# One PSUM tile for each unit, and no product under 64 columns, in a stacked RWKV-7 and mixture-of-experts kernel

## The chip, the cores and the metric

The kernel runs on one core of a Trainium2 chip. The metric is the device time of one execution in microseconds (us). Engines are called as in the profile: PE is the tensor engine's products, PEld its weight loads, DVE the vector engine, ACT the scalar engine, POOL the general engine, SP the engine that issues most transfers. [...]

## The reference

Two blocks run one after the other. The first is a linear recurrence over 768 tokens with 4 batches x 8 heads of dimension 40, and the second sends each token through one of 8 experts.

```python
# attention: for every token t, batch b and head h (state is 40 x 40)
y[t]  = r[t] @ state
Sa    = state @ a[t]
state = state * w[t][:, None] - outer(Sa, b[t]) + outer(v[t], k[t])
# bridge: x = y of all heads side by side, 3072 rows of 320
# experts
logits = x @ w_gate                      # 8 experts
e = argmax(logits); gate = softmax(logits)[e]
out = gate * (relu(x @ w1[e]) @ w2[e])   # hidden size 1024
```

## The kernel before

Tokens are taken in 12 steps of 64. In a step the recurrence becomes a set of small matrix products and a triangular system, which is solved by five doubling levels. The 32 (batch, head) pairs are held as two **units** (`s` = 0, 1) of 16 each: 8 groups `g` times 2 halves `par` of the partitions. A set of products for one unit is therefore 16 products, and since a float32 product leaves two records in the trace, 32 records.

Two streams are woven on PE. `systems` prepares the triangular systems of the next step; `rest` finishes the current step. After every two system products some products of `rest` are issued, in proportion. [...]

```python
def chain(u):                                   # systems, one unit
    return ([lambda: gram(u, 0), lambda: gram(u, 1)] + [lambda k=k: level(u, k) for k in range(5)]
            + [lambda: couple(u), lambda: whole(u)])

def rest(us, nx, before):                       # us: both units of this step
    ps = [right(us), solve(us)] + [lambda u=u: zgram(u) for u in us]
    if before: ps += [(emit(before),)]          # rows of x and logits of the step before
    ps += [lambda u=u: atv(u) for u in nx]
    if not last: ps += [(state(us),)]
    ps += [y_state(us), (y_rest(us),)]
    if not last: ps += [turned(us)]
    return ps
```

PSUM tiles come from two rings of two double banks each: `wide` for the systems (and, with the other tag, for z and atv), `banks` for pairs of smaller results. One call of `banks` allocates one tile and hands out its two halves, one for each unit.

```python
def wide(name, tag="sys"):
    t = pp.tile([128, 2, 512], F32, name=name, tag=tag, bufs=2)
    return t[:].rearrange("q b (g x) -> q (b g) x", x=128)

def banks(name, w):
    t = pp.tile([128, 2, 512], F32, name=name, tag="rest", bufs=2)
    return [t[:, i, : G * w].rearrange("q (g x) -> q g x", x=w) for i in range(2)]

def parted(ps):                                 # PE waits until its writes so far have landed
    nc.scalar.copy(seen[64:65], ps[64:65, G - 1, 0:1])
```

The users of `banks` have the form of `right`, which makes q from two sums of products. The sums come from different halves of the array's rows into the same bank[...].

```python
def right(us):
    pss = banks("ps_q", D)
    for u, ps in zip(us, pss):
        ...
        if c:
            yield [lambda g=g, par=par: mm(
                ps[own(par), g, :], d["ai"][own(par, D), g, :T2], st_r[s][0][own(par, D), g, :D],
                start=(g == 0), stop=False, free=True) for g, par in HD], lambda ps=ps: parted(ps)
    for u, ps in zip(us, pss):
        def end():
            t = d["q"] = q_r[s][0]
            nc.scalar.activation(t[:, :, :D], ps[:], AF.Copy, scale=-1.0)
        yield [lambda g=g, par=par: mm(
            ps[own(par), g, :], d["GT"][oth(par), g, :], d["vu"][par][oth(par), g, :D],
            start=(c == 0), free=True) for g, par in HD], end
# solve (ps_uT), state (ps_s), turned (ps_S), y_state + y_rest (ps_y), emit (ps_x): likewise
```

Evacuations that matter: gram is read by DVE (`pair`) and then ACT (`off`, `nkb`, `GT`); a level by ACT (`pair`), DVE adds, and DVE transposes the copy into the next level's weights `N`; z and atv by four ACT copies each; the levels end with `D`, a DVE transpose that the coupling product `couple` needs.

```python
def zgram(u):                                   # atv has the same form
    ps = wide("ps_z", "rest")
    ts = [lambda g=g, par=par: mm(ps[own(par), g, : T2 + D], d["uT"][oth(par, D), g, :], d["ri"][oth(par, D), g, :])
          for g, par in HD]
    def end():
        for par in range(2):
            nc.scalar.copy(d["vu"][par][own(par), :, :D], ps[own(par), :, T2 : T2 + D])
        for par in range(2):
            t = d["az"][par]
            nc.scalar.copy(t[own(par)], ps[own(par), :, :T2])
            nc.gpsimd.tensor_tensor(t[:], t[:], up64[:, None, :].to_broadcast([128, G, T2]), op=ALU.mult)
    return ts, end
```

The expert block follows, with PSUM tiles of its own; the change does not touch it.

Of the kernel before, what the change touches and what calls it, by code (L numbers as in the profile page):

```python
# [21 lines left out]
def kernel(  # L22
# [102 lines left out]
    with tc.tile_pool(name="ring", bufs=1) as ring, \  # L125
# [16 lines left out]
        def oth(par, n=T2):  # L142
            return slice((1 - par) * 64, (1 - par) * 64 + n)
# [51 lines left out]
        def preset_rest():  # L195
            for s in range(NB2):
                nc.gpsimd.memset(off_r[s][0][:], 0.0)
                nc.gpsimd.tensor_copy(ri_r[s][0][:, :, T2:], i40[:, None, :].to_broadcast([128, G, D]))
                nc.gpsimd.tensor_copy(x_r[s][0][:], i64[:, None, :].to_broadcast([128, G, T2]))

            for t in [r[i] for i in range(2) for r in nkb_r[0] + nkb_r[1] + vu_r[0] + vu_r[1]] + [r[0] for r in q_r + st_r + s_r]:
                nc.gpsimd.memset(t[:, :, D:], 0.0)
            for s in range(NB2):
                nc.gpsimd.memset(kb_r[s][1][:], 0.0)
                for r in (ai_r, ri_r):
                    nc.gpsimd.tensor_copy(r[s][1][:, :, T2:], i40[:, None, :].to_broadcast([128, G, D]))
# [8 lines left out]
                    iw[own(par, D), :, 2 * D :], moe_w_gate.rearrange("(p a e) x -> a e p x", p=NP, a=2)[par],  # L215
                )

        def wide(name, tag="sys"):

            t = pp.tile([128, 2, 512], F32, name=name, tag=tag, bufs=2)  # L220
            return t[:].rearrange("q b (g x) -> q (b g) x", x=128)

        def banks(name, w):

            t = pp.tile([128, 2, 512], F32, name=name, tag="rest", bufs=2)
            return [t[:, i, : G * w].rearrange("q (g x) -> q g x", x=w) for i in range(2)]

        def mm(out_, lhs, rhs, start=True, stop=True, free=False):
            nc.tensor.matmul(out_, lhsT=lhs, rhs=rhs, start=start, stop=stop, skip_group_check=free)  # L229
# [103 lines left out]
        def atv(u):  # L333

            c, s = u
            d = units[u]
            ps = wide("ps_atv", "rest")
            ts = [lambda g=g, par=par: mm(ps[oth(par), g, : T2 + D], d["v"][oth(par, D), g, :], d["ri"][oth(par, D), g, :])
                  for g, par in HD]

            def end():
                d["vu"], d["az"] = [vu_r[par][s][c % 2] for par in range(2)], stack("az", s, T2)
                for par in range(2):
                    nc.scalar.copy(d["vu"][par][oth(par), :, :D], ps[oth(par), :, T2 : T2 + D])
                for par in range(2):
                    nc.scalar.copy(d["az"][par][oth(par)], ps[oth(par), :, :T2])
            return ts, end


# [16 lines left out]
        def level(u, k):  # L366
            c, s = u
            d = units[u]
            ps = wide("ps_lv")
            N, pair = d["N"], d["pair"]  # L370
            rhs = d["nt0"] if k == 0 else pair[:] if k < 4 else pair[:, 2:]
            at = slice(0, T2) if k == 0 else slice(0, T2 + 32) if k < 4 else slice(T2, T2 + 32)
            ts = [lambda g=g, par=par: mm(
                ps[own(par), g, at].rearrange("q (a t) -> q a t", t=32), N[own(par), g].rearrange("q a t -> q (a t)"), rhs[own(par), :, g, :])
                for g, par in HD]

            def end():
                new = pair if k == 0 else new_pair(d, s)
                if k < 4:
                    nc.scalar.copy(parts(new[:, :2]), ps[:, :, :T2].rearrange("q g (a t) -> q g a t", a=2))  # L380
                    new_n(d, s, new[:, :2])
                if k > 0:
                    nc.vector.tensor_tensor(new[:, 2], ps[:, :, T2 : T2 + 32], pair[:, 2], op=ALU.add)
                if k == 4:
                    D_ = d["D"] = sb.tile([128, 1, G, 32], F32, name=f"D{s}")
                    nc.vector.transpose(flat(D_[:]), flat(new[:, 2:]))
                    t = d["TT"] = sb.tile([128, 2, G, 32], F32, name=f"TT{s}")
                    nc.gpsimd.tensor_tensor(
                        t[:], new[:, 2:].to_broadcast([128, 2, G, 32]), blk[:, :, None, :].to_broadcast([128, 2, G, 32]),
                        op=ALU.mult,  # L390
                    )
            return ts, end

        def couple(u):

            c, s = u
            d = units[u]
            ps = wide("ps_y21")
            ts = [lambda g=g, par=par: mm(ps[own(par), g, :32], d["off"][own(par), g, :], d["D"][own(par), 0, g, :])
                  for g, par in HD]  # L400

            def end():
                x = d["x"] = x_r[s][0]
                for par in range(2):
                    qs = slice(par * 64 + 32, par * 64 + 64)
                    nc.scalar.copy(x[qs, :, :32], ps[qs, :, :32])
            return ts, end
# [16 lines left out]

        def right(us):

            pss = banks("ps_q", D)
            for u, ps in zip(us, pss):
                c, s = u
                d = units[u]  # L430
                if c:
                    yield [lambda g=g, par=par: mm(
                        ps[own(par), g, :], d["ai"][own(par, D), g, :T2], st_r[s][0][own(par, D), g, :D],
                        start=(g == 0), stop=False, free=True) for g, par in HD], lambda ps=ps: parted(ps)
            for u, ps in zip(us, pss):
                c, s = u
                d = units[u]

                def end():
                    t = d["q"] = q_r[s][0]  # L440
                    nc.scalar.activation(t[:, :, :D], ps[:], AF.Copy, scale=-1.0)  # L441
                yield [lambda g=g, par=par: mm(
                    ps[own(par), g, :], d["GT"][oth(par), g, :], d["vu"][par][oth(par), g, :D],
                    start=(c == 0), free=True) for g, par in HD], end

        def solve(us):
# [11 lines left out]
        def zgram(u):  # L458

            c, s = u  # L460
            d = units[u]
            ps = wide("ps_z", "rest")
            ts = [lambda g=g, par=par: mm(ps[own(par), g, : T2 + D], d["uT"][oth(par, D), g, :], d["ri"][oth(par, D), g, :])
                  for g, par in HD]

            def end():
                for par in range(2):
                    nc.scalar.copy(d["vu"][par][own(par), :, :D], ps[own(par), :, T2 : T2 + D])
                for par in range(2):
                    t = d["az"][par]  # L470
                    nc.scalar.copy(t[own(par)], ps[own(par), :, :T2])  # L471
                    nc.gpsimd.tensor_tensor(t[:], t[:], up64[:, None, :].to_broadcast([128, G, T2]), op=ALU.mult)  # L472
            return ts, end

# [16 lines left out]

        def turned(us):

            for u, ps in zip(us, banks("ps_S", D)):
                c, s = u

                def end():
                    nc.scalar.copy(s_r[s][0][:, :, :D], ps[:])
                yield [lambda g=g, par=par: mm(ps[oth(par), g, :], st_r[s][0][own(par, D), g, :], i40[own(par, D), :])
                       for g, par in HD], end  # L500

        def y_state(us):
# [21 lines left out]

        def emit(us):

            for u, ps in zip(us, banks("ps_x", 2 * NP * D // G + 2 * E)):
                c, s = u
                d = units[u]
                ps = ps.rearrange("t g x -> t (g x)")[:, : NP * (2 * D + E)].rearrange("t (p x) -> t p x", p=NP)  # L530

                def end():
                    xr = sb.tile([128, DX], F32, name="xr", bufs=2)
                    lg = sb.tile([128, E], F32, name="lg", bufs=2)
                    nc.scalar.copy(xr[:, :Dm].rearrange("t (p e) -> t p e", p=NP), ps[:, :, : 2 * D])  # L535
                    nc.gpsimd.tensor_copy(xr[:, Dm:], xr[:, Dm - 64 : Dm])
                    nc.vector.tensor_reduce(lg[:], ps[:, :, 2 * D :].rearrange("t p x -> t x p"), axis=AX, op=ALU.add)  # L537
                    nc.vector.tensor_scalar_mul(lgn[:, s * NS + c, :], lg[:], -1.0)
                    for b2 in range(2):
                        r0 = (2 * s + b2) * S + c * T2  # L540
                        nc.sync.dma_start(
                            x_d[r0 : r0 + T2, :DX], xr[b2 * 64 : b2 * 64 + 64],
                        )
                yield [lambda p=p, b2=b2: mm(ps[b2 * 64 : b2 * 64 + 64, p, :], d["y"][:, b2 * NP + p, :], iw[:, p, :])
                       for p in range(NP) for b2 in range(2)], end
# [431 lines left out]
```

## Time and profile before

| what | value |
|---|---|
| time, median of 3 | 1018.59 us (1015.94 to 1034.52) |
| profiled execution | 1026.1 us |
| recurrence, until its last product | about 725 us |
| expert products, from the first gather on | from about 745 us |
| granted PE clock, mean | 0.83 of full |
| ACT copies of z and atv | 64x512: 579 to 580 ns, 64x320: 419 to 420 ns, 48 of each kind |

The profile is of one execution. "Busy" of PE counts records from start to end, and records overlap, so that a busy PE need not be at its peak; how close starts of records follow each other is the better measure. A clock of 0.50 means that PE ran at half rate in that stretch. A wait is put down to the last event that released it. The largest groups of PE by product, from the list of groups:

```profile
L229 PE MATMUL ps_gram<-ai,kb 40*64 40x104 f32 x1536 | 197.9, 367 | 27.8 <-POOL ai L282 24.3 <-POOL kb L291 3.6
L229 PE MATMUL ps_lv<-pair,N 64*64 64x96 f32 x2304 | 151.7, 265 | 14.4 <-ACT az L471 10.3 <-DVE N L357 2.2 <-DVE pair L383 1.1
L229 PE MATMUL ps_q<-vu,GT 64*64 64x40 f32 x768 | 86.6, 300 | 8.8 <-ACT q L441 8.5 <-ACT seen L236 0.3
L229 PE MATMUL ps_q<-st,ai 40*64 40x40 f32 x704 | 67.2, 257 | 21.9 <-ACT seen L236 21.9
```

A row gives the tile written and those read, rows x weight columns, rows x columns moved, the number of records, busy us and mean ns, and after the second bar the idle time before the group and what ended it.

### The profile page before, as it was taken

To read this page: it belongs to the slowest core of one execution; us is meant where nothing else is said; L and a number is where in the kernel's file an instruction comes from. 1 tells how busy PE (TensorE), PEld (TensorE's weight loads), DVE (VectorE), ACT (ScalarE), POOL (GpSimd) and SP (SyncE) were. 2 spreads that over 40 slices of the span, in tenths; PEclk is the share of its full clock that TensorE was granted. 3 is DMA by queue.
4 is the path that set the end of the run, shared out by engine and by line. 5 is a ranking of instruction groups with operands and counts; after the bars stand their busy time and mean duration, and the time that the engine had idled before them with its cause. 6 is when DMAs were issued, how large, how long until landed. Compare 5 with 4: busy or idle time off the path is not lost. (4 is left out here: it accounts for less than half of the span.)

```text
span 1026.1 us, 33566 instructions
## 1 busy us (share of the span) xinstructions
PE 857.3 (84%) x14960; PEld 705.1 (69%) x14960; DVE 370.6 (36%) x642; ACT 320.0 (31%) x704; POOL 349.2 (34%) x395
## 2 busy tenths in 40 slices
PE   0778888888888888888888888888369999999996
PEld 0668887787778887877877787877235555555554
DVE  2552726263544527262635446240620111011100
ACT  0233525262535325362625344443001111111110
POOL 9542525171615325251616144222242121221011
PEclk9975958788796759788787859695569999999998
DMA  3211302112121212121121201000652252422100
GB/s 88 47 35 43 76 11 61 44 44 51 32 61 34 57 34 47 43 51 39 45 51 31 54 3 45 3 19 18 209 156 92 67 190 74 164 80 80 60 19 20
DMA packets 123365, 60.95 MB, mean 59 GB/s; under 512 B 103697, under 2 KB 119059, under 8 KB 123220
## 3 DMA queue, kind: packets, MB, share of 16 engines
q1 hardware_dynamic: 112868, 48.34, 18.0%
q0 software_dynamic: 3136, 9.46, 3.1%
q8 instruction: 118, 1.93, 0.8%
q10 hardware_dynamic: 7216, 1.00, 0.6%
q14 instruction: 27, 0.22, 0.1%
HBM read 50.09 MB, written 9.32 MB: 58 GB/s over the span
## 5 line engine op out<-in xcount | busy, mean ns | idle before, releaser
L229 PE MATMUL ps_lv<-pair,N 64*64 64x96 f32 (+2 forms) x3840 | 230.5, 266 | 21.2 <-ACT az L471 10.3
L229 PEld LDWEIGHTS ps_lv<-pair,N 64*64 64x64 f32 x3840 | 205.9, 156 | 26.6 <-issue 19.8
L229 PE MATMUL ps_gram<-ai,kb 40*64 40x104 f32 x1536 | 197.9, 367 | 27.8 <-POOL ai L282 24.3
L229 PEld LDWEIGHTS ps_gram<-ai,kb 40*64 40x64 f32 x1536 | 149.6, 194 | 28.2 <-POOL ai L282 24.3
L867 PE MATMUL zp<-w,h_sb 128*128 128x320 f32 (+1 forms) x512 | 124.1, 433 | 0.0
L357 DVE STREAM_TRANSPOSE N<-pair 128x512 f32<-128x512 f32 x120 | 84.5, 704 | 100.2 <-ACT pair L380 99.2
L312 DVE TENSOR_TENSOR pair<-ps_gram,nup 64x512 f32<-64x512 f32 x48 | 33.1, 689 | 230.9 <-PE ps_gram L229 230.9
L867 PEld LDWEIGHTS zp<-w,h_sb 128*128 128x128 f32 (+1 forms) x512 | 80.4, 177 | 37.2 <-issue 2.4
L291 POOL TENSOR_TENSOR kb<-kb,wi 128x512 f32<-128x512 f32 x48 | 61.8, 1287 | 123.1 <-DVE wi L288 112.8
L851 PE MATMUL hp<-xgT,w 128*128 128x448 f32 x256 | 102.4, 553 | 0.0
L872 POOL DMA_INDIRECT out_dram<-zo,s_idx x28 | 27.9, 998 | 209.7 <-ACT zo L871 189.2
L325 POOL TENSOR_TENSOR pair<-pair 128x256 f32<-128x256 f32 x24 | 17.5, 727 | 234.5 <-DVE pair L312 234.5
L857 DVE TENSOR_SCALAR h_sb<-hp 128x448 f32<-128x448 f32 x32 | 20.0, 625 | 210.2 <-PE hp L851 133.0
L229 PEld LDWEIGHTS ps_q<-vu,GT 64*64 64x64 f32 x768 | 84.8, 210 | 14.9 <-ACT q L441 12.0
L229 PE MATMUL ps_q<-vu,GT 64*64 64x40 f32 x768 | 86.6, 300 | 8.8 <-ACT q L441 8.5
L288 DVE RECIPROCAL wi<-PT 128x128 f32<-128x128 f32 x96 | 88.6, 928 | 0.1
L229 PE MATMUL ps_q<-st,ai 40*64 40x40 f32 x704 | 67.2, 257 | 21.9 <-ACT seen L236 21.9
L851 PEld LDWEIGHTS hp<-xgT,w 128*128 128x128 f32 x256 | 48.1, 193 | 53.8 <-issue 53.8
L472 POOL TENSOR_TENSOR az<-az,up 128x512 f32<-128x512 f32 x48 | 69.1, 1460 | 43.7 <-ACT az L471 43.6
L229 PEld LDWEIGHTS ps_q<-st,ai 40*64 40x64 f32 x704 | 63.9, 166 | 24.3 <-ACT seen L236 24.3
L229 PE MATMUL ps_atv<-ri,v 40*64 40x104 f32 x768 | 72.0, 257 | 0.9 <-ACT az L471 0.5
L229 PE MATMUL ps_uT<-F,q 64*64 64x64 f32 x768 | 59.5, 316 | 12.7 <-ACT uT L454 12.7
(173 smaller groups left out, 1361.0 us busy)
## 6 DMA issues: line engine op xcount, KB each, us to landing
w<-in_moe_w_dram SPq DMA_DIRECT2D x8, 1280.0 KB
w<-in_moe_w_dram SPq DMA_DIRECT2D x8, 1024.0 KB
kb<-in_packed_dram SPq DMA_DIRECT2D x176, 40.0 KB
x_rows<-xr SPq DMA_DIRECT2D x48, 96.0 KB
v<-in_packed_dram SPq DMA_DIRECT2D x96, 40.0 KB
wp<-in_packed_dram SPq DMA_DIRECT2D x96, 40.0 KB
ri<-in_packed_dram SPq DMA_DIRECT2D x96, 40.0 KB
a<-in_packed_dram SPq DMA_DIRECT2D x88, 40.0 KB
```

What stands on the lines that cost most here:

```text
L229: nc.tensor.matmul(out_, lhsT=lhs, rhs=rhs, start=start, stop=stop, skip_group_check=free)
L288: nc.vector.reciprocal(wi[:, h, p : p + 2], by_batch(d["PT"][:, :, 1:])[:, h, p : p + 2])
L291: nc.gpsimd.tensor_tensor(kb, kb, wi[:, h, :, None, :].to_broadcast([128, NP, 2, T2]), op=ALU.mult)
L312: nc.vector.tensor_tensor(parts(nt)[own(par)], ps[own(par), :, :T2].rearrange("q g (a t) -> q g a t", a=2), nup[own(par)].rearrange("q (a ...
L325: nc.gpsimd.tensor_tensor(new[:, 2], old[:, 0], old[:, 1], op=ALU.add)
L357: nc.vector.transpose(N[:].rearrange("q g a t -> q a g t"), nt)
L472: nc.gpsimd.tensor_tensor(t[:], t[:], up64[:, None, :].to_broadcast([128, G, T2]), op=ALU.mult)
L851: nc.tensor.matmul(hps[a][:, :cols], lhsT=w[0][:, db, f0 : f0 + 128], rhs=xT[:, db, :cols], start=(q % 2 == 1 and db == 0), stop=(q % 2 == ...
L857: nc.vector.tensor_relu(h[:, 2 * q, :cols], hps[0][:, :cols])
L867: nc.tensor.matmul(zp[i * n : i * n + n], lhsT=h[:, fb, c0 : c0 + n], rhs=w[2][:, fb, :], start=(fb == 0), stop=(fb == FB - 1),)
L872: ins_ = nc.gpsimd.indirect_dma_start(out=out[:, :], out_offset=bass.IndirectOffsetOnAxis(ap=idx, axis=0), in_=zo[:], in_offset=None, boun ...
```

## The change

It does two things in the recurrence.

- The PSUM of all but the systems becomes a ring of four single banks. `banks` now allocates one tile for each unit. z and atv, which need two banks, take two tiles of four groups each (`halves`), and their ACT copies are cut accordingly, from four to eight. It is meant to let each bank be waited for and freed by itself.
- No product of the recurrence moves fewer than 64 columns. q and the transposed state S move 64 instead of 40, the last level and the coupling 64 instead of 32. The added columns are padding, or are moved twice, and nobody reads them. The scheduling order of the products on PE stays.

```diff
-        def wide(name, tag="sys"):
-            t = pp.tile([128, 2, 512], F32, name=name, tag=tag, bufs=2)
+        def wide(name):
+            t = pp.tile([128, 2, 512], F32, name=name, tag="two", bufs=2)
             return t[:].rearrange("q b (g x) -> q (b g) x", x=128)

-        def banks(name, w):
-            t = pp.tile([128, 2, 512], F32, name=name, tag="rest", bufs=2)
-            return [t[:, i, : G * w].rearrange("q (g x) -> q g x", x=w) for i in range(2)]
+        def bank(name, w, gs=G):
+            return pp.tile([128, gs, w], F32, name=name, tag="one", bufs=4)
+        def halves(name):
+            ps = [bank(name, T2 + D, NP) for _ in range(2)]
+            return ps, lambda h, g: ps[g // NP][h, g % NP, :]
+        def banks(name, w, gs=G):
+            return [bank(name, w, gs) for _ in range(2)]
 ... zgram (atv likewise)
-            ps = wide("ps_z", "rest")
-            ts = [lambda g=g, par=par: mm(ps[own(par), g, : T2 + D], ...
+            ps, at = halves("ps_z")
+            ts = [lambda g=g, par=par: mm(at(own(par), g), ...
-                for par in range(2):
-                    nc.scalar.copy(d["vu"][par][own(par), :, :D], ps[own(par), :, T2 : T2 + D])
-                for par in range(2):
-                    t = d["az"][par]
-                    nc.scalar.copy(t[own(par)], ps[own(par), :, :T2])
+                for h in range(2):
+                    gs = slice(h * NP, h * NP + NP)
+                    for par in range(2):
+                        nc.scalar.copy(d["vu"][par][own(par), gs, :D], ps[h][own(par), :, T2:])
+                        nc.scalar.copy(d["az"][par][own(par), gs], ps[h][own(par), :, :T2])
+                for t in d["az"]:
                     nc.gpsimd.tensor_tensor(t[:], t[:], up64[:, None, :].to_broadcast([128, G, T2]), op=ALU.mult)
 ... level: the last one moves 64 columns
-            rhs = d["nt0"] if k == 0 else pair[:] if k < 4 else pair[:, 2:]
+            rhs = d["nt0"] if k == 0 else pair[:] if k < 4 else pair[:, 1:]
 ... couple: D moved twice
-            ts = [lambda g=g, par=par: mm(ps[own(par), g, :32], d["off"][own(par), g, :], d["D"][own(par), 0, g, :])
+            ts = [lambda g=g, par=par: mm(
+                ps[own(par), g, :T2].rearrange("q (a t) -> q a t", a=2), d["off"][own(par), g, :],
+                d["D"][own(par), :, g, :].to_broadcast([64, 2, 32]))
 ... right (turned likewise, with i64 for i40)
-            pss = banks("ps_q", D)
+            pss = banks("ps_q", 64)
-                        ps[own(par), g, :], d["ai"][own(par, D), g, :T2], st_r[s][0][own(par, D), g, :D],
+                        ps[own(par), g, :], d["ai"][own(par, D), g, :T2], st_r[s][0][own(par, D), g, :],
-                    ps[own(par), g, :], d["GT"][oth(par), g, :], d["vu"][par][oth(par), g, :D],
+                    ps[own(par), g, :], d["GT"][oth(par), g, :], d["vu"][par][oth(par), g, :],
 ... emit: banks of four groups of 88 columns
```

## The prediction, before the changed kernel ran

> **What bounds the kernel now.** I read the page first (busy shares and granted clock), then busy time by stretch over one step, then who waited for whom on the tensor engine, then the timeline at the spots that these pointed to. The page and the stretches:
>
> ```profile
> PE 857.3 (84%) x14960; PEld 705.1 (69%) x14960; DVE 370.6 (36%) x642; ACT 320.0 (31%) x704; POOL 349.2 (34%) x395
> ...
> PEclk9975958788796759788787859695569999999998
> ```
>
> ```profile
> 420.00:423.40 3.40, 1.23 (x35) 1.18 (x35) 0.68 (x1) 1.31 (x4) 0.00 (x0) 1.00 0.19 44
> 423.40:433.60 10.20, 9.64 (x139) 9.07 (x135) 2.54 (x4) 2.99 (x8) 0.97 (x2) 0.50 0.15 34
> 433.60:443.90 10.30, 9.16 (x231) 8.97 (x228) 6.11 (x8) 4.42 (x10) 7.59 (x7) 0.50 0.23 51
> 443.90:474.60 30.70, 25.86 (x800) 23.85 (x794) 17.43 (x32) 15.17 (x34) 13.73 (x12) 1.00 0.21 48
> ```
>
> PE is the busiest engine and no other passes 36%. In the second fence each row is a stretch: its length, then the busy time and count of PE, PEld, DVE, ACT and POOL, then the granted clock. It is one of the twelve 64-token steps, 54.6 us. PE is busy 1.23 us in the first 3.4 us, and then the clock is halved for 20.5 us although PE works nearly all of that time. So a step loses in two ways: PE stands idle, and PE runs at half clock. The same happens from step to step (the first ps_uT records of successive steps start at 434.8, 489.5 and 544.4). Who PE waited for:
>
> ```profile
> PE ps_q L229 <- ACT seen L236: 22.2, 12, 2.2
> PE ps_uT L229 <- ACT uT L454: 12.7, 12, 1.1
> ...
> PE ps_x L229 <- DVE lg L537: 11.0, 12, 1.5
> PE ps_lv L229 <- ACT az L471: 10.3, 10, 1.1
> PE ps_S L229 <- ACT s L498: 9.6, 11, 0.9
> PE ps_q L229 <- ACT q L441: 8.5, 12, 2.4
> PE ps_y L229 <- DVE D L386: 8.3, 11, 1.1
> ...
> PE ps_s L229 <- DVE acc L485: 6.9, 10, 0.7
> ```
>
> Columns: total us, times, longest. Each comes 10 to 12 times, once a step. Six of the eight name an operation that reads the same PSUM tile as the waiting product writes: `seen` and q read ps_q, uT reads ps_uT, lg reads ps_x, s reads ps_S, acc reads ps_s. In the code these products run for two units, and `banks` gives both units the two halves of ONE tile. The second unit's first product therefore waits until the first unit's half has been read, though it writes the other bank. ps_lv<-az and ps_y<-D are not of this kind.
>
> [...] 0.50 and 1.00 alone within the stretches above, and the drop follows the 3.4 us in which PE was busy for 1.23. [...] (half clock, start, us, count):
>
> ```profile
> 351.38 1.92 PE L229 MATMUL ps_y<-D,off 64*64 64x32 f32 x32
> 353.23 1.97 PE L229 MATMUL ps_y<-az,nkb 128*64 128x64 f32 x32
> ```
>
> Thirty-two records of 32 columns take 1.92 us, thirty-two of 64 columns 1.97. [...]
>
> **The change, part by part.**
>
> *Shared tiles removed.* Around 400 to 460 us the gaps of over 0.25 us on PE in one step are: s 0.69, D 0.78, S 0.90, q (`seen`) 2.17, q 0.56, uT 1.14, lv<-az 1.07, x 0.88 = 8.2 us. Of these s, S, both q, uT and x (6.3 us) are the shared-tile waits. With a tile for each unit they have no cause. The ring is no shorter: four single banks come round as often as two double ones, and each bank is free as soon as its own reader is done.
>
> *Wider products.* q, ps_S (40 to 64 columns), level 4 and the coupling ps_y (32 to 64). Each product leaves two records. In a step these are 64+64 q, 64 S, 64 level 4, 64 coupling. If time followed columns at 29.2 ns for 64 (spacing of 64-column records alone at full clock), it would cost 192x24x0.456 + 128x32x0.456 = 4.0 us a step. But 40-column S beside 64-column f, and 32-column level 4 beside 64-column ps_y, are spaced 14.6 ns a record, which is what 26.7 ns of 64-column uT beside 64-column level 0 at half clock come to (13.4 doubled). So I book zero. What they do is raise the array's activity. I sorted the 3.41 us windows of the stacked stage by rows fed x columns moved, summed over their records, in units of 128 rows. Almost all drops followed a window under about 1920, and nearly no other window was under it. The window at 420 has 745. q (from st) beside gram without a gap (36.9 ns a record) would give 92 records x 40/128 x (104+40)/2 = 2080, hardly above the line; with 64 columns, 2420. This line is my estimate from this trace alone.
>
> *Halved evacuations.* atv and z now need 8 ACT copies instead of 4. From 579 ns (512 columns) and 420 (320), a column costs 0.83 ns and a copy 153 fixed, so 256 columns take 366 (the 32x256 copy xt has 364) and 160 take 287. 4x287+4x366 = 2.61 us instead of 2x420+2x579 = 2.00: +0.61 us, four times a step, +2.4 us ACT a step. ACT has 23.9 us in 54.6, so it stays under PE; but the level copies `pair` queue behind the z copies (the 1.07 us wait). I book +1.5 us a step on the path, with the tighter chain below.
>
> *The sum for one step at full clock.* Spacing per record read off record starts, times records:
>
> - gram + q: 256 x 36.8 ns = 9.4 us (at half clock 70.0)
> - uT + level 0: 128 x 14.6 = 1.9
> - z + level 1: 128 x 22.3 = 2.9
> - atv + level 2: 128 x 43.4 = 5.6
> - x: 32 x 47.3 = 1.5
> - s + level 3: 128 x 44.6 = 5.7
> - y_state + level 4: 128 x 14.6 = 1.9
> - y_rest: 64 x 35 = 2.2
> - coupling: 64 x 29.2 = 1.9
> - S + f: 128 x 14.6 = 1.9
>
> Stream 34.9 us. Check on before: 34.9 + 8.2 of gaps + half of the 18.8 us that PE was busy at half clock = 52.5 of 54.6, leaving 2.1 for short waits. After: 34.9 + (8.2-6.3) + 2.1 + 1.5 = 40.4 us if the clock stays, so 14 us less a step. The eleven intervals between first ps_uT records (89.1 to 698.4) average 55.4, some being longer, so 15.0 each: 165 us. Two of eleven steps may still lose the clock, 9.4 each: +19. The ends of the stage (before 89, after 698) have a few such waits: -5. The expert stage from 745 us on is untouched. 1018.6 - 165 + 19 - 5 = 868.
>
> **The rivals.**
> 1. *The waits go, the clock does not come back* (gram feeds only 40 rows). For it: the window at 344.9 us has 92 records and still led to a drop. Against: those were narrow ps_y and level-4 products of 40 rows and 32 columns, which the change widens. Then only 11 x (6.3-1.5) = 53 us go: about 965.
> 2. *A wait of another kind takes the place.* At full clock a gram piece takes 64 x 36.8 = 2.4 us, and its evacuation (DVE 0.69, then ACT 0.37, 0.40, 0.58, overlapping, from 302.1 to 304.1) 2.0, so a bank of the two-deep `two` ring is free only just in time. Level 0 with uT lasts 32+32 records = 0.95 us a unit, while its copy (0.58) and transpose (0.70) need 1.4 with the hand-overs. If that costs 5 us more a step: about 920.
> 3. *The wide products or the ACT copies eat the gain.* By the columns 4.0 us a step, plus 2.4 of ACT in full on the path: 70 us back on 868, so 940. The 1.92 against 1.97 us speaks against the first half.
> 4. *DMA.* The packed loads are 21% of the DMA engines in this step and would be 28%; the page's waits have one DVE scan that waited 1.9 us for wp. I expect nothing.
>
> **Range and chances.** Most of the gain rests on the clock, which is all or nothing for a step: between 838 (no drop, smaller gaps) and 930 (rival 2, or half of the steps dropping) I see 8 chances in 10. Faster by over 2% 0.93, within 2% 0.04, slower 0.03: even with rival 1 the shared-tile waits alone are 5%.
>
> **What would show it.** Right: ps_q<-seen, ps_uT<-uT, ps_x<-lg, ps_S<-s, ps_s<-acc gone from PE's waits or under 3 us each; granted clock 1.00 through most steps; steps of about 40 us; 64-column records in the same 14.6 and 29.2 ns. Wrong: a step of 48 us or more with the clock still halved at gram and q (rival 1); PE waits for DVE N, DVE pair or ACT pair/GT above 3 us a step (rival 2); gram beside q over 40 ns a record at full clock (rival 3).

## The result, and the profile after

| | before | after |
|---|---|---|
| time, median of 4 runs each | 1020.7 us | 863.6 us (856.8 to 874.4) |
| ratio, 95% interval | | 0.845 [0.836, 0.854] |
| profiled span | 1026.1 us | 866.9 us |
| granted PE clock, mean | 0.83 | 0.945 |
| first ps_uT record of the first and the last step | 89.1 and 698.4 us | 85.7 and 553.6 us |

The eleven intervals between these records give 141.4 us of the 159.2 us by which the two profiled spans differ. The stretch ahead of them gives 3.4 and that behind them 14.4. The page of the changed kernel:

```profile
PE 745.6 (86%) x14960; PEld 607.1 (70%) x14960; DVE 366.4 (42%) x642; ACT 328.6 (38%) x896; POOL 348.7 (40%) x395
...
PEclk9996799999999999979789999966999999999999
```

The number of PE records is unchanged. The row of sevens, eights and fives that ran through the recurrence in the clock before is now a row of nines with two dips (slice 18, and slices 20 and 21, of 21.7 us each), apart from the start and the end of the stage. In the clock records of both profiles the clock is 1.00 or 0.50, and every stretch of one clock but the last is a whole number of times 3.41 us long, 1 to 76 of them before and 1 to 77 after; that length is what I call a window. ACT does 896 operations in place of 704 and is busy for only 9 us more. One step by stretch (length, then busy time and count of PE, PEld, DVE, ACT and POOL, then the clock):

```profile
290.90:294.30 3.40, 2.43 (x67) 2.22 (x66) 0.03 (x1) 0.71 (x2) 0.00 (x0) 1.00 0.06 14
294.30:300.60 6.30, 6.30 (x180) 6.29 (x173) 2.76 (x5) 3.88 (x12) 0.62 (x1) 1.00 0.31 70
300.60:310.80 10.20, 7.67 (x300) 6.93 (x297) 8.07 (x11) 8.70 (x26) 10.04 (x10) 1.00 0.25 55
310.80:332.90 22.10, 20.02 (x651) 18.86 (x651) 15.51 (x30) 11.05 (x33) 11.54 (x11) 1.00 0.29 66
```

The first two rows are gram beside q: 9.7 us at full clock, where before it was 3.4 us at full and more than 10 us at half. The third row is where a step now loses most: PE is busy for 7.7 of 10.2 us, and ACT for 8.7 and POOL for 10.0. What PE waits for (total us, times, longest):

```profile
PE ps_lv L237 <- DVE pair L392: 18.1, 24, 1.9
PE ps_y L237 <- DVE D L395: 13.7, 13, 1.3
PE ps_lv L237 <- ACT GT L327: 11.5, 10, 1.5
...
PE ps_lv L237 <- DVE N L366: 7.8, 12, 1.7
...
PE ps_q L237 <- issue: 4.5, 4, 1.5
```

The six waits on a shared tile are gone from the list; what is left is the chain of the levels themselves (copy, add, transpose) and the bank that gram's last copy frees. The last line is new: four waits of q, about every third step, that the profile puts to no engine. At full clock, records of 64 columns follow each other nearly as those of 32 did (start, us; the first line is the coupling of the kernel before, with 32 columns, and the others are of the changed kernel, the coupling and then y_rest):

```profile
412.35 1.12 PE L229 MATMUL ps_y<-D,off 64*64 64x32 f32 x32
286.41 1.15 PE L237 MATMUL ps_y<-D,off 64*64 64x64 f32 x32
287.49 1.15 PE L237 MATMUL ps_y<-az,nkb 128*64 128x64 f32 x32
```

The coupling takes 1.15 us in place of 1.12, as long as y_rest beside it. Gram beside q is at about 36.5 ns a record from start to start with q at 64 columns, as it was at 40.

### The profile page after: what moved, and what is told of

It is laid out like the page before. It is cut to its first block, busy times and chain, and to the rows that moved or that the text cites. A ratio compares the mean times of both kernels' runs of the same rounds, so it can differ in the third digit from the quotient of the medians.

```text
span 866.9 us, 33816 instructions
## 1 busy us (share of the span) xinstructions
PE 745.6 (86%) x14960; PEld 607.1 (70%) x14960; DVE 366.4 (42%) x642; ACT 328.6 (38%) x896; POOL 348.7 (40%) x395
## 4 chain that ended last, share of the span: by engine, by line
PE 36%; issue 31%; DVE 13%; POOL 8%; ACT 6%; DMA 4%; SPq 1%; POOLq 0%; DVEq 0%; ACTq 0%
PE ps_gram L237 9%; PE ps_lv L237 6%; PE ps_y L237 6%; PE ps_atv L237 5%; PE ps_q L237 4%; POOL out_dram L883 3%; DVE N L366 3%; PE ps_f L237 2%; DVE pair L392 2%; ACT pair L389 2%; DVE PT L286 2%; DVE wi L296 1%; POOL xg L830 1%; DMA kb<-in_packed_dram 1%; ACT az L482 1%
## 5 line engine op out<-in xcount | busy, mean ns | idle before, releaser
L237 PE MATMUL ps_lv<-pair,N 64*64 64x96 f32 (+1 forms) x3840 | 200.3, 244 | 37.7 <-DVE pair L392 18.1
L237 PEld LDWEIGHTS ps_lv<-pair,N 64*64 64x64 f32 x3840 | 180.9, 140 | 46.4 <-ACT GT L327 14.9
L237 PE MATMUL ps_gram<-ai,kb 40*64 40x104 f32 x1536 | 141.4, 298 | 28.3 <-POOL ai L290 24.3
L237 PEld LDWEIGHTS ps_gram<-ai,kb 40*64 40x64 f32 x1536 | 112.7, 156 | 28.9 <-POOL ai L290 24.3
L333 POOL TENSOR_TENSOR pair<-pair 128x256 f32<-128x256 f32 x24 | 17.5, 730 | 147.3 <-DVE pair L320 147.2
L389 ACT COPY pair<-ps_lv 128x512 f32<-128x512 f32 x96 | 56.5, 589 | 37.1 <-issue 15.3
L869 ACT ACTIVATE h_sb<-hp 128x448 f32<-128x448 f32 x32 | 17.4, 544 | 140.0 <-PE hp L862 84.9
L237 PE MATMUL ps_atv<-ri,v 40*64 40x104 f32 x768 | 69.4, 256 | 0.0
L237 PE MATMUL ps_q<-vu,GT 64*64 64x64 f32 x768 | 63.1, 252 | 0.0
L237 PEld LDWEIGHTS ps_q<-vu,GT 64*64 64x64 f32 x768 | 60.1, 153 | 0.2
L237 PEld LDWEIGHTS ps_atv<-ri,v 40*64 40x64 f32 x768 | 58.4, 136 | 1.0
```

The costliest lines, as they stand in the source:

```text
L333: nc.gpsimd.tensor_tensor(new[:, 2], old[:, 0], old[:, 1], op=ALU.add)
```

## The experiments

Ten variants were timed, and one of them and the changed kernel a second time. Except for `seam_wait` and `evac_more`, which add an idle copy, all do the same computation in another form.

**The two parts alone.** `ring_only` has the ring of single banks and the old widths, `wide_only` the old double banks and the new widths.

```diff
# ring_only, against the changed kernel (right; likewise turned, couple, the last level)
-            pss = banks("ps_q", 64)
+            pss = banks("ps_q", D)
-    ... d["ai"][own(par, D), g, :T2], st_r[s][0][own(par, D), g, :],
+    ... d["ai"][own(par, D), g, :T2], st_r[s][0][own(par, D), g, :D],
# wide_only: the opposite edits, in the kernel before
```

> The changed kernel with every product at its old width (q and S 40 columns, last level and coupling 32); the ring of four single banks stays. My theory (the shared-tile waits cost time, the padding lifts the activity at gram and q over the line that keeps the clock): the shared-tile waits stay gone, but gram beside 40-column q gives about 2080 in a 3.4 us window against a line of about 1920, so small gaps halve the clock in about half of the steps; about 905 us (880 to 930). Rival A (the padding does nothing): 863, within 10 us. Rival B (the padding is what keeps the clock): every step drops at gram and q, about 960 us or more.

> The kernel before with the wider products alone; two double banks for both units as before. My theory: the shared-tile waits stay at 6.3 us a step, the 3.4 us window with the 2.17 us wait holds some 17 records of q whose 24 more columns add only about 130 to its 700, so the clock is still halved in each step: 1000 to 1025 us, that is within 2% of before. Rival B (the padding alone keeps the clock): 11 x 9.4 us less, about 915. Rival C (wide products cost by the column): 44 us more, about 1060.

Measured: `ring_only` 898.0 us (884 to 900), ratio to before 0.875 [0.868, 0.883]; `wide_only` 1008.3 us (1007.4 to 1009.7), ratio 0.981 [0.973, 0.990]. Both fall in the range of the theory. The ring alone brings most of the gain, and the widths alone about 2%, with the seam as it was before:

```profile
241.20:244.60 3.40, 1.23 (x35) 1.03 (x34) 0.68 (x1) 1.31 (x4) 0.00 (x0) 1.00 0.21 48
244.60:265.10 20.50, 18.80 (x356) 18.01 (x357) 7.55 (x10) 7.07 (x16) 8.11 (x8) 0.50 0.19 42
```

The widths on top of the ring bring 21 to 34 us: the changed kernel was not timed beside `ring_only`, and its two timings gave 863.6 and, later, 877.0. In `ring_only` one seam reads (the two last lines are of a later step):

```profile
303.50:306.90 3.40, 2.43 (x109) 2.23 (x102) 0.00 (x0) 1.83 (x4) 0.00 (x0) 1.00 0.08 19
306.90:310.30 3.40, 3.40 (x100) 3.39 (x95) 0.68 (x1) 1.32 (x5) 0.00 (x0) 1.00 0.25 57
310.30:324.00 13.70, 13.47 (x278) 13.29 (x279) 6.93 (x9) 6.38 (x15) 7.28 (x7) 0.50 0.23 52
...
446.90:450.30 3.40, 3.40 (x98) 3.38 (x95) 1.06 (x2) 1.46 (x5) 0.00 (x0) 1.00 0.29 65
450.30:453.70 3.40, 3.40 (x100) 3.40 (x95) 1.53 (x3) 2.22 (x6) 0.42 (x1) 1.00 0.27 61
```

In the second row PE is busy for the whole 3.40 us, with gram beside 40-column q at full clock, and right after it the clock is halved for 13.7 us. So in this run the clock does not follow idle time alone. In my unit (rows fed x columns moved, summed over the records and divided by 128) this window has 2145. But the window from 446.9 us has the same products, the same 3.40 us of busy PE and about the same sum, and after it the clock stays at full. The sum of this window lies where both happen; it gives no sharp line.

**The padding of q alone.**

```diff
# the four q edits of ring_only alone, in the changed kernel; S, last level and coupling stay at 64
```

> The changed kernel with q alone back at 40 columns; S, last level and coupling stay at 64. My theory puts the weakest spot at gram beside q, so this behaves as the kernel with all products narrow, within 15 us of it. Rival: the padding counts where all products are narrow (S, last level, coupling), and this stays within 10 us of 863.

Measured: 886.9 us, but from 870 to 901, ratio 0.851 [0.840, 0.861]. The ratio leaves out runs more than 1.5% above the fastest of their kernel, so that it lies below what the median would give. The median is within the 15 us of `ring_only` that the theory allowed, while the interval overlaps that of the changed kernel (0.836 to 0.854), which speaks for the rival. The runs differ by their clock: the run of 870 us was granted 0.939 of it, that of 901 us 0.898. Which windows the clock was lost after, between the first and the last ps_uT record, shows that both paddings count:

| profile | drops after a window of gram and q, or of q | drops after other windows |
|---|---|---|
| `ring_only` | 5 | 5, with the last level, the coupling or S |
| `q_narrow` | 8 | 0 |
| changed kernel, two profiles | 2 and 3 | 1 and 2, with uT beside level 0 |

With q narrow the drops come at gram and q alone; where the last level, the coupling and S are narrow too, they come there as well. How the microseconds divide between them stays open.

**One wait put back.**

```diff
# seam_wait, in right(), against the changed kernel
+            def held(ps, s):
+                parted(ps)
+                if s == 0:
+                    nc.scalar.copy(st_r[1][0][0:1, 0, 63:64], ps[0:1, G - 1, 0:1])
-                        start=(g == 0), stop=False, free=True) for g, par in HD], lambda ps=ps: parted(ps)
+                        start=(g == 0), stop=False, free=True) for g, par in HD], lambda ps=ps, s=s: held(ps, s)
```

The element written is padding that only reaches unread columns.

> The changed kernel with one of the six waits put back: after the copy that ends the first q products of unit 0, ACT also writes one padding element of the operand that unit 1's first q product reads, so that product waits for it as it did before (2.17 us a step); one more ACT copy of one element a step. My theory: this one wait empties the window and halves the clock for the gram and q that follow, so it costs 2.2 + about 9.4 us in each of 11 steps: about 985 us (950 to 1000). Rival (a wait costs only itself): 11 x 2.2 = 24 us, about 888.

Measured: 937.5 us (935 to 945), ratio 0.912 [0.904, 0.920]: between the two predictions, 74 us over the changed kernel's 863.6 (60 over its second timing). The wait as PE's list has it, and one seam by stretch:

```profile
PE ps_q L237 <- ACT st L443: 23.8, 11, 2.3
```

```profile
274.40:277.80 3.40, 0.93 (x20) 0.65 (x16) 0.68 (x1) 1.02 (x3) 0.00 (x0) 1.00 0.23 53
277.80:294.90 17.10, 16.36 (x306) 16.17 (x309) 5.62 (x8) 6.24 (x17) 6.57 (x7) 0.50 0.17 39
```

The wait itself is 23.8 us, as the rival said, and the clock then falls at every seam, as the theory said. Steps grow from 42.5 to 49.5 us on average: 2.2 of wait and, for the rest, 4.8 of clock, not 9.4. Between the first and the last ps_uT record the half-clock time grows from 46.8 to 185.6 us, so it costs less than half of itself. A part of the reason is that the slower PE also waits less here: PE's wait for gram's last copy is 3.5 us in this profile against 11.5 in the changed kernel's.

**Rows in place of columns.** If the clock follows rows fed x columns moved, it must answer to rows too. Gram feeds 40 rows of a 64-row tile, and the other 24 rows of its operands hold zeros already, so they can be fed at no change of the result.

```diff
# rows_narrow: in ring_only; rows_wide: in the changed kernel, with the same for the first q product
-                ps[i * 64 : i * 64 + 64, g, : T2 + D], d["kb"][own(par, D), g, i, :], d["ai"][own(par, D), g, :])
+                ps[i * 64 : i * 64 + 64, g, : T2 + D], d["kb"][own(par), g, i, :], d["ai"][own(par), g, :])
```

> The ring with the narrow products (898 us before), and gram fed 64 rows in place of 40 (rows 40 to 63 of both operands hold zeros, so the result is the same); columns and order as before. My theory (the clock follows rows fed x columns moved): gram beside 40-column q rises from about 2100 to about 2970 a window, far over the line, so the clock stays up and this comes to about 862 us (850 to 875). Rival A (columns alone count, or the values): 898, within 12 us. Rival B (a product of 64 rows takes longer): above 898.

> The changed kernel with gram and the first q product fed 64 rows in place of 40 (zeros). My theory: gram beside q rises from 2420 to about 3870 a window, so the seams that still lost the clock in the changed kernel keep it unless a gap is over 1.7 us: about 850 us (842 to 858). Rival (rows do not count): 863, within 8 us.

Measured: `rows_narrow` 873.8 us (868 to 878), `rows_wide` 849.8 us (846 to 855); both in the theory's range. `rows_narrow` has no wider product than `ring_only` and is 24 us faster, in another session, but with no run in the other's range. Rival B is out: gram beside q is spaced 36.5 ns a record in both. In its profile no drop between the first and the last ps_uT record follows gram and q any more; six follow the last level, the coupling or S, which are still narrow. `rows_wide`, timed again beside the changed kernel on one chip:

> The changed kernel unaltered, timed beside the next one: 863 us, within 8 us.

> The changed kernel with gram and the first q product fed 64 rows, timed beside the unaltered one on the same chip. If the 14 us between them are the clock at the seams and not chance: 850 us, within 8 us, and no half-clock stretch between the second and the eleventh step. Rival (chance): within 6 us of the unaltered one.

Measured: 877.0 us (867 to 888), ratio 0.852 [0.845, 0.859], against 850.1 us (848 to 857), ratio 0.830 [0.825, 0.835]. The intervals are apart, so the version with 64 rows beats both kernels. The unaltered kernel came out 14 us above what I expected. The clock of the version with 64 rows on its page:

```profile
PEclk9999999999999999999999999957999999999998
```

No seam loses the clock for longer than one window of 3.4 us, and even the start of the stage keeps it: the first ps_uT record stands at 78.6 us in place of 84.8. The one short stretch, at 231.6 us, is not the "none" that I had expected. The eleven intervals between first ps_uT records have a mean of 41.2 us, against 43.0 in the profile of the unaltered kernel beside it.

**The ACT copies.** First more of them, then fewer.

```diff
# evac_more, z and atv alike
                         nc.scalar.copy(d["az"][par][own(par), gs], ps[h][own(par), :, :T2])
+                        nc.scalar.copy(d["az"][par][own(par), gs], ps[h][own(par), :, :T2])
# merged: vu and az are halves of one tile; atv alike
-                        nc.scalar.copy(d["vu"][par][own(par), gs, :D], ps[h][own(par), :, T2:])
-                        nc.scalar.copy(d["az"][par][own(par), gs], ps[h][own(par), :, :T2])
+                        nc.scalar.copy(d["both"][par][own(par), gs, : T2 + D], ps[h][own(par)])
```

> The changed kernel with four more ACT copies (64x256, about 0.37 us each) after those of every z and atv, 1.46 us more ACT a set, four sets a step, nothing else. If the copies lie on the path in full: 46 sets x 1.46 = 67 us more, about 930. My theory: those of z do in part, as the next level's copy queues behind them, those of atv do not, as the tensor engine is the slower one there: 1.5 to 3 us a step, 880 to 896. Rival: ACT has room and it costs under 8 us, 863 to 871.

> The changed kernel with the two destinations of every z and atv copy (64 columns and 40) side by side in one tile, so that one ACT copy of 64x416 replaces a 64x256 and a 64x160: four copies a set instead of eight, 4 x (153 + 416 x 0.83) = 2.0 us instead of 2.6, everything else as it is. The run with four copies more showed such copies to lie on the path in full, so this gives back 4 x 0.61 us in each of some 11.5 steps, 28 us: about 836 us (828 to 848). Rival (only added copies hurt; at the changed kernel's own length other waits are as long): 855 or more. Second rival (state products now wait for the mask that POOL puts on the other half of the same tile): slower than 863.

> The same together with gram and the first q product fed 64 rows. If the two gains (28 us and 14 us) are of different kinds, copies on the path and clock, they add: about 822 us (812 to 832). Rival (they share the same waits): no better than 836.

Measured: `evac_more` 932.1 us (924 to 938), 68 us more than 863.6, and `merged` 867.5 us (866 to 871), ratio 0.851 [0.846, 0.857], no gain where I expected 28 us. `merged_rows`, 854.7 us, ratio 0.837 [0.832, 0.843], is no better than the version with 64 rows alone. My milder guess for `evac_more` was too mild, but that the 68 us come near the 67 of the full length does not put the copies on the path in full. Of the 69 us between its profiled span (935.8) and that of the changed kernel (866.9), PE is idle for 46 us more (167.6 against 121.3); for the other 23 it is busy longer with the same 14960 records (768.2 against 745.6), at a granted clock of 0.915 against 0.945. So about two thirds of the added length show as waiting, and the rest is clock. Most of the idle time is the wait for the level's add, 18.1 us before:

```profile
PE ps_lv L237 <- DVE pair L393: 57.6, 36, 2.6
```

In the changed kernel ACT has no idle time in this stretch:

```profile
265.96 0.29 ACT L481 COPY vu<-ps_z 64x160 f32<-64x160 f32 x1
266.15 0.37 ACT L482 COPY az<-ps_z 64x256 f32<-64x256 f32 x1
266.55 0.59 ACT L389 COPY pair<-ps_lv 128x512 f32<-128x512 f32 x1
267.03 0.28 ACT L481 COPY vu<-ps_z 64x160 f32<-64x160 f32 x1
```

The level copy `pair` stands between the copies of two z, without a gap, so that more copies push it back. The lines also show why `merged` had little to give: a copy of 160 columns has 0.29 us, but the next copy starts 0.19 us after it. From first start to last end the eight copies of a set take 2.29 us and the four of `merged` 2.06, so about 0.2 us a set were to be had and not 0.61: ACT is busy for 318.3 us in place of 328.6, 10 us less and not 28. Even these 10 us don't appear in the time. In `merged`, PE's waits move:

```profile
PE ps_lv L239 <- ACT GT L329: 12.2, 12, 1.5
PE ps_lv L239 <- DVE pair L394: 11.9, 18, 2.2
...
PE ps_atv L239 <- DVE lg L549: 4.1, 5, 0.9
```

The wait for the level's add falls from 18.1 to 11.9 us, and a new one of 4.1 us appears, atv on the bank that DVE's `lg` frees. That other waits are about as long here is the likely reason for no gain at all; no run shows it alone.

**DVE work moved.**

```diff
# decay_moved: the items that prepare the step after next, by piece, in place of one each from the third piece on
-                weave(systems(nx) if nx else [], rest(...), 304, ahead, 2)
+                weave(systems(nx) if nx else [], rest(...), 304, ahead, 2, {0: 1, 1: 1, 2: 1, 3: 1, 8: 2, 9: 1, 10: 2, 11: 1})
```

> The changed kernel with the DVE work for the step after next (two scans, eight reciprocals of 0.93 us) taken out of the level 0 and level 1 pieces and put beside gram (one each in the first four pieces) and levels 2 and 3 (six). If DVE's queue behind these reciprocals is what makes the tensor engine wait for the level adds (0.75 us, twice a step) and transposes, 1 to 2 us a step go: 840 to 855. Rival (these waits are the chain of copy and transpose itself, or the evacuation of gram now waits for DVE): 863 or slower.

Measured: 870.9 us (862 to 875): no gain. PE's wait for the add, which this should have cut, is longer in its profile (26.9 us in place of 18.1). Where the reciprocals were taken away, the wait of about 1.0 us in front of level 2 stays in most steps, so that it is not due to them. Where two of them now stand, the wait in front of level 4 grows from 0.54 to 1.35 us in nine of eleven steps. So the run speaks against the reciprocals as the cause of the wait in front of level 2, and shows that DVE has no room for two of them in front of level 4.

## Why the prediction was right

It gave 868 us and a range of 838 to 930; 863.6 were measured, and 877.0 in the second timing. The mechanism held. That the sum came so close is partly luck, as terms were off in opposite directions (see the ends).

- **The shared-tile waits.** All six are gone. `ring_only` shows it without the widths, and a ratio of 0.875. This step held. `ring_only` changes the tile for each unit, the ring of four and the halves of z and atv together; these were not tried apart. `parted` stands in both kernels, and no run leaves it out.
- **Wider products at no cost.** They were booked at zero, and their spacing hardly changed: 1.15 us in place of 1.12 for 32 records of the coupling, and about 36.5 ns a record for q beside gram, as before. `wide_only`, 2% under the runs of the kernel before beside it and not 44 us above, excludes the cost by columns.
- **The clock.** The mechanism held in these runs: `seam_wait` brings the drop back with the wait alone (185.6 us at half clock in place of 46.8), `ring_only` loses the clock with PE busy for 3.40 of 3.40 us, and rows of zeros bring it back in `rows_narrow` (a mean clock of 0.929 against 0.908 in `ring_only`, in the profiles) and `rows_wide` (0.972 against 0.945 in the changed kernel). Two sizes were off. The line at 1920 is none: windows of 2117 to 2224 led to a drop in the kernels with narrow q, and one of about 2150 in `ring_only` did not. Nor does the sum alone decide: the changed kernel lost the clock for 3.4 us after the window from 176.9 us, with a sum of about 2600 in which PE was busy for only 1.72 us. Rows, columns and waits all count in these runs; the exact measure stays open. And a drop costs about 4 to 8 us, not 9.4.
- **The step at full clock.** 40.4 us were predicted; the seven intervals without a long drop have 41.0 to 42.0. The gaps of one step (1.42 at level 0, 0.35, 1.00, 0.54, 1.27 at D, 0.97) come to 5.55 us, against 1.85 + 2.1 + 1.5 = 5.45 predicted; the products themselves take about 1 us more than the 34.9 that I summed. The 1.5 us was put down to the ACT copies and the tighter chain. The copies were mis-sized, since I added durations that overlap: a set takes 2.29 us where it took 2.03, +0.25 and not +0.61, and ACT is busy for 9 us more in the whole run, not 28. That leaves the chain for most of the 1.5 us; it was not tried by itself.
- **Rival 2.** It came true in part. The waits named as its sign (DVE `N`, DVE `pair`, ACT `GT`) together grow from 10.2 to 37.4 us, or 3.1 in each of twelve steps, just over the 3 us that I had set. But they stay within the gaps booked above, and the step did not become 5 us longer.
- **Steps that still lose the clock.** +19 us were booked for two. In the profile three intervals are long (47.8, 45.1, 49.1), together 17.5 us over 41.5. In the longest the clock is lost after a wait of 1.55 us of ps_q, one of the four that the profile puts to no engine. What it is stays open.
- **The ends.** This term was mis-sized: -5 us predicted, -17.8 measured (3.4 ahead, 14.4 behind). I had counted the waits there and left out the clock: behind the last ps_uT the half-clock time falls from 61 us (27.3 and 34.1) to 30.7 in one stretch. Half of the difference, 15 us, is an upper estimate of what the clock gave there; it was not tried apart. The eleven intervals gave 141 us where 165 - 19 = 146 were predicted, and the ends 18 where 5 were. One gained 5 us less than booked and the other 13 more, so that each hides a part of the other: that is the luck in the sum.

## What to carry to other kernels

In this kernel two results in one tile were one buffer for the six waits that the ring removed, 70.9 us in all before. Where the list of waits shows an engine waiting, once per round, for the reader of the other half, give each half its own tile before anything else: `ring_only`, which does so with a ring of four single banks, came to a ratio of 0.875. In `seam_wait` 23.8 us of wait came with 74 us of time (60 by the second timing), as the clock was halved at every seam, so look at the clock after a wait, not only at the wait. Where products use part of a tile's rows or columns and time does not depend on them (here gram beside q had 36.5 ns a record with 40 rows and with 64), feeding the unused ones with zeros can keep the clock up for nothing, as the 850.1 in place of 877.0 us show.

## What was unexpected of the hardware

In `ring_only` the clock was halved after a 3.40 us window in which PE was busy for 3.40 us (gram of 40 rows beside q of 40 columns), though not after the one from 446.9 us, as busy and with the same products. With gram fed 64 rows, of which 24 were zeros, and the same columns, no drop followed gram and q in the profile of `rows_narrow`. Gram beside q had 36.5 ns a record there. So a busy PE alone was not enough here to keep the clock, and the rows fed counted, rows of zeros too: 873.8 us in place of 898.0. The columns moved counted as well: 8 drops followed gram and q in the profile of `q_narrow`, and 2 and 3 in those of the changed kernel.
